# Three mantissa bits of each weight word by ScalarE into a PSUM bank, and a new table of ranks

## The chip, the core and the metric

One Trainium2 chip, one core. The metric is the device time of one execution in microseconds (us). On the core TensorE (PE) multiplies into PSUM, VectorE (DVE), ScalarE (ACT) and GpSimd (POOL) do the elementwise work, and SyncE (SP) issues nearly all the transfers. PSUM has eight banks of 512 fp32 numbers for each of 128 partitions.

## The reference, cut to what matters

```python
# attention over 32 memory rows per head: q, k, v, phi are (4, 8, 576, 64 or 32)
a = softmax(phi, axis=2)
k_m = einsum('bhsm,bhsd->bhmd', a, k);  v_m = einsum('bhsm,bhsd->bhmd', a, v)
attn = softmax(q @ k_m.T / sqrt(64));   x = (attn @ v_m) as (2304, 512)
# a gated layer, d_ff 1536; its three weights arrive as 64-bit floats
g = x @ moe_w_gate
x = (g * sigmoid(g) * (x @ moe_w_val)) @ moe_w_out
# eight experts, each token goes to the one with the highest logit
e = argmax(x @ moe2_w_gate);  out[i] = gate_w[i] * (relu(x[i] @ w1[e]) @ w2[e])
```

The first weights, `moe_w_gate`, `moe_w_val` and `moe_w_out`, are drawn as doubles. The kernel gets each as two 32-bit words and has to make an fp32 number of them. The change is in that step.

## The kernel before, in words

Every product runs in three passes: an operand is cut into a rounded high part and a rest (`cut`, line 424: the high part by ACT, line 427, the rest by DVE or POOL, line 429), and high times high, high times rest and rest times high are added in PSUM.

The program has three parts. First, for batches 0 to 3, memory rows from `phi` (tile `ph`), `k` and `v` (tile `kvraw`), then scores against `q` (tile `qt`): PE makes `kvp` (line 535), `pt` (574) and `psc` (622); DVE turns, reduces and normalises the scores (lines 643 to 672) in a tile `sA` and leaves `af`, which `cut` turns into `at`. Second, the gated layer, in 12 column groups `ft` of 128 columns in both weights: PE multiplies the weight tile `wgv` with the memory rows `tv` into `pm` (818); `cut` makes `mh` of it; PE multiplies `mh` with `at` into `pg` and `pv` (920), a pair for each half batch; DVE and ACT make the gated `sg` and `gh`; PE multiplies `gh` with the output weight `wo` into `py` (964). Third, experts in units of 288 tokens, `p` (1480 and 1520), to the end. Batches 0 and 1 go through the gated layer first, 2 and 3 after them with weights stored and reloaded.

The weights come in 36 chunks of 512 KB (24 of `wgv`, two for each column group, 12 of `wo`). SP brings a chunk into a tile `wr` (line 723), 512 pairs of words for each partition. `words` (line 726) makes 512 fp32 numbers in the tile `mag` of it:

- line 733, ACT: reads the high word as fp32 and scales it by 2^-111, so that sign, exponent and 20 mantissa bits stand three bits too far right in `mag`;
- line 735, DVE: the sign bit of `mag`, into the high word of `wr`;
- line 737, DVE: the low word of `wr` shifted right by 29 (three mantissa bits), joined with that;
- line 739, DVE: `mag` shifted left by three, joined with it, into `mag`;
- then `cut`: ACT makes the high part of the weight tile, POOL the rest.

There are four `wr` tiles and two `mag` tiles, and `wr` is free after line 739.

The order of the work on each engine is not written out. A planner (`Loom`) runs the program as threads on a model of the engines when the kernel is built, and issues an instruction when its thread is chosen; among threads that are ready on an engine the lower rank goes first. The table `RANK` holds these ranks, for loads, conversions, scores, products and so on. The planner's costs of an instruction are `on_v`, `on_v2`, `on_a`, `on_g`, `on_pe` and `on_dma`; `on_v2` marks a DVE instruction with two operands in SBUF, for which the model lets POOL and DVE slow each other. `banks` are the eight PSUM banks, and a thread that wants one waits in the plan until one is free.

Of the kernel before, what the change touches and what calls it, by code (L numbers as in the profile page):

```python
# [9 lines left out]
F32R = mybir.dt.float32r  # L10
BF16 = mybir.dt.bfloat16
I32 = mybir.dt.int32
AF = mybir.ActivationFunctionType
ALU = mybir.AluOpType
AX = mybir.AxisListType
# [3 lines left out]


RANK = {
    "gate": -427.7, "mh": -121.7, "mem": -6.5, "mem0": -3.9, "py": 225.9, "out": 216.2, "tables": 206.8, "warm": -9,
# [5 lines left out]
    "mh1": -125.4, "py1": 5.2, "turn": -32.0, "route": -35.0, "zeros": -96.4, "lists": -142.7, "marks": -35.9, "pick": 100.3,  # L28
# [3 lines left out]
}  # L32


class Event:
    def __init__(self):
        self.time, self.waiting = None, []
# [12 lines left out]
class Loom:  # L50
# [5 lines left out]
    def __init__(self, slack=0.0, look=100.0):  # L56
        self.slack, self.look, self.table, self.shared = slack, look, AF.Exp, 0.0
        self.busy = dict.fromkeys(("PE", "V", "A", "G", "SP", "DMA"), 0.0)
# [101 lines left out]
def on_v(n, half=False):  # L160
    return "V", 0.06 + n * (0.00053 if half else 0.00105)


def on_v2(n, half=False):
    return *on_v(n, half), True


def on_a(n, table=None):
    cost = 0.11 + n * 0.00104
    return ("A", cost, table) if table else ("A", cost)  # L170


def on_g(n):
    return "G", 0.3 + n * 0.0021
# [6 lines left out]
def on_dma(kb):  # L181
    return "SP", kb / 340
# [14 lines left out]
def attention_moe_moe_kernel(  # L197
# [14 lines left out]
    nc = tc.nc  # L212
# [30 lines left out]
    def bank(name):  # L243
        return ps.tile([128, 512], F32, tag="bank", name=name, bufs=8)
# [7 lines left out]
    def wraw(shape, name, dt=F32):  # L252
        return sb.tile(shape, dt, tag="wr", name=name, bufs=4)
# [4 lines left out]
    def t2k(shape, name, dt=F32):  # L258
        return sb.tile(shape, dt, tag="t2k", name=name, bufs=2)
# [69 lines left out]
    def tables():  # L329

        cap_i = sb.tile([128, 1], I32, name="cap_i")
        rg32 = sb.tile([128, NDT, E], F32, name="rg32")
        yield atts[0].phq[0]
        yield on_dma(20)
        nc.sync.dma_start(cap_i, capacity.bitcast(I32)[0:1].partition_broadcast(128))
        yield on_dma(60)
# [4 lines left out]
        yield t2k_s  # L341
        ints = t2k([128, 512], "ints", I32)
        parts, at = [], 0
# [73 lines left out]
    loom = Loom(RANK["slack"], RANK["look"])  # L417
    banks = Slots(8)
# [6 lines left out]
    def cut(src, hi, lo, n, pool=False):  # L425
        yield on_a(n)
        nc.scalar.activation(hi, src, AF.Copy)  # L427
        yield on_g(n) if pool else on_v(n)
        (nc.gpsimd if pool else nc.vector).tensor_sub(lo, src, hi.bitcast(F32))  # L429

    class Attention:
# [67 lines left out]
        def powers(self, Q):  # L499
# [4 lines left out]
            nc.vector.tensor_reduce(sums[:, 0:1], ph[:, Q], AX.X, ALU.max, negate=True)  # L504
            yield "A", 0.95, AF.Exp
            nc.scalar.activation(ph[:, Q], ph[:, Q], AF.Exp, bias=sums[:, 0:1], accum_out=sums[:, 1:2])
            yield self.ex_ready
# [92 lines left out]
        def scores(self, n):  # L600
# [48 lines left out]
            nc.vector.tensor_sub(s2, s1, m1.unsqueeze(2).to_broadcast([128, 2 * NK, MM]))  # L649
            yield on_a(2 * NB, AF.Exp)  # L650
            nc.scalar.activation(s1, s2, AF.Exp, scale=float(D) ** -0.5)
            m2 = sb.tile([128, 2 * NK], F32, tag="m1", name="m2", bufs=4)
# [65 lines left out]
    def convert(raw_ap, dst, key, chunk, kb, rank):  # L718

        yield wr_s  # L720
        raw = wraw([128, raw_ap[1], 2], "wr", I32)
        yield on_dma(kb)
        nc.sync.dma_start(raw.rearrange("p f w -> p (f w)"), raw_ap[0])
        loom.spawn(words(raw, dst, key, chunk), rank, loom.landed)

    def words(raw, dst, key, chunk):
        low, high = raw[:, :, 0], raw[:, :, 1]
        n = raw.shape[1]
        yield mag_s
        mag = sb.tile([128, n], F32, tag="mag", name="mag", bufs=2)  # L730
        val = mag.bitcast(I32)
        yield on_a(n)
        nc.scalar.activation(mag, high.bitcast(F32), AF.Copy, scale=2.0**-111)
        yield on_v2(n, True)
        nc.vector.tensor_scalar(high, val, -(1 << 31), None, ALU.bitwise_and)
        yield on_v2(n)
        nc.vector.scalar_tensor_tensor(high, low, 29, high, ALU.logical_shift_right, ALU.bitwise_or)
        yield on_v2(n)
        nc.vector.scalar_tensor_tensor(val, val, 3, high, ALU.logical_shift_left, ALU.bitwise_or)
        loom.put(wr_s)  # L740
        hi, lo = dst
        src = mag.rearrange("p (a b) -> p a b", b=hi.shape[-1]) if len(hi.shape) == 3 else mag
        yield from cut(src, hi, lo, n, pool=True)
        loom.put(mag_s)
        loom.set(wparts[key][chunk])
# [3 lines left out]
    def weights(key, rank):  # L749

        yield w8_s
        if isinstance(key, int):
            w = wtiles[0, key] = w8([128, 2, NDT, 2, 128], "wgv")
            for i in range(2):
                src = w_gv[key, i].bitcast(I32)
                yield from convert((src, NDT * 128), (w[:, 0, :, i], w[:, 1, :, i]), key, i, 524, rank)
# [951 lines left out]
    tv_ready, turn, pair = Event(), Slots(1), Slots(1)  # L1708
# [113 lines left out]
```

## Time and profile before

| | us |
|---|---|
| median of 3 runs | 704.24 |
| lowest and highest | 702.95, 707.14 |
| the profiled execution | 702.52 |
| its span, first to last instruction | 700.7 |
| PE busy in the span | 653.9 |
| DVE, ACT, POOL busy | 455.6, 366.2, 237.0 |

The profiled execution took 1.8 us more than its span. PE is busy for 93% of the span; what it is not busy with adds up to 46.8 us. [...] In a row of the order in time, brackets at the end give how long the engine stood idle before the piece and what released it.

### The profile page before, as it was taken

What the parts mean: (1) busy time and instruction counts of PE and PEld (TensorE: products, weight loads), DVE (VectorE), ACT (ScalarE), POOL (GpSimd) and SP (SyncE); (2) the same over time, 40 slices, a digit from 0 to 9 for tenths busy, and PEclk for the clock granted to TensorE, in tenths of its full rate; (3) what the DMA queues carried; (4) which work ended last, traced back from release to release, by engine and by line L of the source; (5) the groups of instructions that cost most, each with busy time, mean ns of one, the idle gap of its engine ahead of it and who ended that gap; (6) DMA issues with size and microseconds to landing.
All of it is one profiled execution on the core that took longest, in us unless ns stands there. A gap on an engine that the chain in (4) does not pass through costs nothing. (4 is left out here: it accounts for less than half of the span.)

```text
span 700.7 us, 12589 instructions
## 1 busy us (share of the span) xinstructions
PE 653.9 (93%) x4681; PEld 600.6 (86%) x4681; DVE 455.6 (65%) x948; ACT 366.2 (52%) x695; POOL 237.0 (34%) x217
## 2 busy tenths in 40 slices
PE   5399899999999899999999999999999999999993
PEld 4198698898898789889988988889899999999982
DVE  4998987499988767813624656873663854854633
ACT  4556767777477556634613743433454543743531
POOL 3444674265536222301711320004641632421302
PEclk9689899999999999999999999999999999999998
DMA  9975667677574416245933533434955856655341
GB/s 355 384 305 214 196 240 256 226 249 235 200 308 166 185 61 211 63 179 150 308 122 124 195 102 106 121 92 101 288 147 185 249 133 218 190 158 201 109 167 38
DMA packets 48737, 132.04 MB, mean 188 GB/s; under 512 B 7648, under 2 KB 16864, under 8 KB 44064
## 3 DMA queue, kind: packets, MB, share of 16 engines
q1 hardware_dynamic: 45440, 121.44, 51.1%
q0 software_dynamic: 3232, 9.74, 4.5%
q8 instruction: 39, 0.64, 0.4%
q14 instruction: 26, 0.21, 0.1%
HBM read 98.10 MB, written 33.33 MB: 188 GB/s over the span
## 5 line engine op out<-in xcount | busy, mean ns | idle before, releaser
L964 PE MATMUL py<-wo,gh 128*128 128x512 f32 x648 | 157.0, 396 | 2.4 <-POOL wo L429 2.4
L964 PEld LDWEIGHTS py<-wo,gh 128*128 128x128 f32 x648 | 120.4, 190 | 27.0 <-POOL wo L429 3.2
L429 POOL TENSOR_TENSOR gh<-sg,gh 128x288 fp32r<-128x288 f32 x96 | 84.3, 885 | 170.7 <-ACT gh L427 165.7
L1520 PE MATMUL p<-hh,w2h 128*128 128x288 f32 x768 | 113.3, 299 | 0.2 <-issue 0.2
L1480 PE MATMUL p<-xt,w1h 128*128 128x288 f32 x768 | 110.6, 297 | 0.6 <-DVE xt L429 0.6
L1520 PEld LDWEIGHTS p<-hh,w2h 128*128 128x128 f32 x768 | 104.3, 189 | 0.5 <-ACT xt L427 0.3
L1480 PEld LDWEIGHTS p<-xt,w1h 128*128 128x128 f32 x768 | 104.0, 189 | 0.9 <-DVE xt L429 0.8
L287 POOL DMA_INDIRECT out_dram<-ot,idx x24 | 54.4, 2265 | 131.0 <-DVE ot L1559 127.9
L920 PE MATMUL pg<-at,mh 128*128 128x288 f32 x576 | 95.7, 301 | 2.0 <-POOL at L429 0.7
L920 PE MATMUL pv<-at,mh 128*128 128x288 f32 x576 | 92.9, 298 | 0.0
L920 PEld LDWEIGHTS pg<-at,mh 128*128 128x128 f32 x576 | 82.3, 190 | 6.9 <-DVE mh L429 2.0
L920 PEld LDWEIGHTS pv<-at,mh 128*128 128x128 f32 x576 | 82.2, 190 | 0.8 <-issue 0.4
L429 DVE TENSOR_TENSOR mh<-pm,mh 64x512 fp32r<-64x512 f32 (+1 forms) x88 | 60.3, 685 | 24.7 <-ACT mh L427 22.8
L833 DVE SCALAR_TENSOR_TENSOR sg<-sg,pv 128x288 f32<-128x288 f32 x96 | 42.5, 449 | 40.0 <-ACT sg L830 19.9
L427 ACT ACTIVATE mh<-pm 64x512 fp32r<-64x512 f32 (+1 forms) x88 | 51.9, 590 | 24.1 <-PE pm L818 18.9
L1496 DVE SCALAR_TENSOR_TENSOR hh<-p,hh 128x288 fp32r<-128x288 f32 x64 | 28.7, 449 | 53.6 <-ACT hh L1494 52.7
L1494 ACT ACTIVATE hh<-p 128x288 fp32r<-128x288 f32 x64 | 26.2, 409 | 68.8 <-PE p L1480 62.6
L427 ACT ACTIVATE gh<-sg 128x288 fp32r<-128x288 f32 x96 | 41.7, 442 | 34.4 <-DVE sg L833 33.2
L818 PE MATMUL pm<-wgv,tv 128*128 128x256 f32 x336 | 49.2, 292 | 10.1 <-ACT wgv L427 9.0
L429 DVE TENSOR_TENSOR w2h<-w2r,w2h 128x1024 fp32r<-128x1024 f32 x36 | 43.6, 1216 | 21.7 <-ACT w2h L427 21.7
L818 PEld LDWEIGHTS pm<-wgv,tv 128*128 128x128 f32 x336 | 44.4, 195 | 14.5 <-ACT wgv L427 9.9
L1432 POOL DMA_INDIRECT xr<-x,idg x24 | 27.0, 1123 | 73.1 <-DVE idx L1343 64.0
(205 smaller groups left out, 863.8 us busy)
## 6 DMA issues: line engine op xcount, KB each, us to landing
w1r<-in_moe_w_dram SPq DMA_DIRECT2D x36, 512.0 KB
w2r<-in_moe_w_dram SPq DMA_DIRECT2D x36, 512.0 KB
wr<-in_moe_w_gv_dram SPq DMA_DIRECT2D x24, 512.0 KB
wsc<-wgv SPq DMA_DIRECT2D x12, 1024.0 KB
wgv<-wsc SPq DMA_DIRECT2D x12, 1024.0 KB
kvraw<-in_kv_dram SPq DMA_DIRECT2D x16, 640.0 KB
wr<-in_moe_w_out_dram SPq DMA_DIRECT2D x12, 512.0 KB
osc<-wo SPq DMA_DIRECT2D x6, 1024.0 KB
```

The lines of the kernel that those rows point to most:

```text
L287: ins = nc.gpsimd.indirect_dma_start(*args, **kwargs)
L427: nc.scalar.activation(hi, src, AF.Copy)
L429: (nc.gpsimd if pool else nc.vector).tensor_sub(lo, src, hi.bitcast(F32))
L818: nc.tensor.matmul(pm[:, Q * 256 : (Q + 1) * 256], tv[:, 2 * Q + hp, a, :], w[:, c, 2 * Q + hp], start=(k == 0 and n3 == 0), stop=(k == le ...
L833: nc.vector.scalar_tensor_tensor(sg, sg, 2.0**-16, pv[:, :NB], ALU.mult, ALU.mult)
L920: nc.tensor.matmul(pg[:, :NB], mh[:, a, Q, gv * 128 : gv * 128 + 128], at[:, Q, c, ns], start=(Q == 0 and n3 == 0), stop=(Q == 1 and n3 == 2),
L964: nc.tensor.matmul(py, gh[:, a, k * TC : (k + 1) * TC], wtiles[P, ws[j // 2]][:, j % 2, c, :], start=(j == 0 and n3 == 0), stop=(j == FG - ...
L1432: nc.gpsimd.indirect_dma_start(self.xr[:, c], None, x2[: NT // 2] if self.early else x2, bass.IndirectOffsetOnAxis(idg[:, c : c + 1], 0))
L1480: nc.tensor.matmul(p1[:, :NB], self.w1[d][:, a, f * 128 : f * 128 + 128], self.xt[d][:, c], start=(d == 0 and n3 == 0), stop=(d == NDT - 1 ...
L1494: nc.scalar.activation(dst[:, 0], p1[:, :NB], AF.Relu)
L1496: nc.vector.scalar_tensor_tensor(dst[:, 1], p1[:, :NB], 0.0, dst[:, 0].bitcast(F32), ALU.max, ALU.subtract)
L1520: nc.tensor.matmul(p2[:, :NB], self.w2[f // 2][:, f % 2, a, d * 128 : d * 128 + 128], self.hh[f][:, c], start=(f == 0 and n3 == 0), stop=( ...
```

## The change

In `words` three DVE instructions become two and ACT gets a second one. ACT reads the upper 16 bits of the low word as an unsigned integer (`top`, one element of 2 bytes out of each 8), scales it by 2^-13 with a bias that makes the rounding a rounding down, and writes the three bits as integers into a PSUM bank, `rest`. DVE joins the sign bit of `mag` to `rest` in PSUM, then `mag` shifted left by three with `rest` into `mag`. The `wr` tile is free when ACT has read it; the conversion holds one of the eight banks from the ACT instruction to the second DVE instruction. In the planner both DVE instructions are `on_v`. The `RANK` table is replaced as a whole, so that the order of all engines is another. The rows of the table say nothing to a reader; two stand for them.

```diff
-        low, high = raw[:, :, 0], raw[:, :, 1]
+        high = raw[:, :, 1]
...
-        yield on_v2(n, True)
-        nc.vector.tensor_scalar(high, val, -(1 << 31), None, ALU.bitwise_and)
-        yield on_v2(n)
-        nc.vector.scalar_tensor_tensor(high, low, 29, high, ALU.logical_shift_right, ALU.bitwise_or)
-        yield on_v2(n)
-        nc.vector.scalar_tensor_tensor(val, val, 3, high, ALU.logical_shift_left, ALU.bitwise_or)
+        yield banks
+        rest = bank("rest")[:, :n].bitcast(I32)
+        top = raw.rearrange("p f w -> p (f w)").bitcast(U16).rearrange("p (f w) -> p f w", w=4)[:, :, 1]
+        yield on_a(n)
+        nc.scalar.activation(rest, top, AF.Copy, bias=2.0**-14 - 0.5, scale=2.0**-13)
         loom.put(wr_s)
+        yield on_v(n)
+        nc.vector.scalar_tensor_tensor(rest, val, -(1 << 31), rest, ALU.bitwise_and, ALU.bitwise_or)
+        yield on_v(n)
+        nc.vector.scalar_tensor_tensor(val, val, 3, rest, ALU.logical_shift_left, ALU.bitwise_or)
+        loom.put(banks)
...
 RANK = {
-    "0ph": -128.5, "0kv0": -121.3, "0kv1": -56.1, "0q0": 48.4, "0q1": -118.9, "0m0": 109.9, "0m1": -64.4, "0s0": -159.6,
...
+    "0ph": -162.0, "0kv0": -136.0, "0kv1": -377.0, "0q0": 181.1, "0q1": -139.4, "0m0": 136.5, "0m1": -351.5, "0s0": -381.1,
...
```

Three places of the new order. The first is SP at the very start: `ph_105` is `phi` of batch 0, `ph_115` of batch 1, `kvraw` are the four parts of `k` and `v` of batch 0. Before:

```order
L723 DMA wr_112<-in_moe_w_gv_dram 128x1024
L723 DMA wr_121<-in_moe_w_gv_dram 128x1024
L453 DMA ph_105<-in_phi_dram 128x576 x2
L473 DMA kvraw_106<-in_kv_dram 128x1280
L473 DMA kvraw_131<-in_kv_dram 128x1280
L496 DMA qt_108<-in_q_dram 128x1152
L453 DMA ph_115<-in_phi_dram 128x576 x2
```

And now:

```order
L724 DMA wr_112<-in_moe_w_gv_dram 128x1024
L724 DMA wr_121<-in_moe_w_gv_dram 128x1024
L474 DMA kvraw_107<-in_kv_dram 128x1280
L474 DMA kvraw_125<-in_kv_dram 128x1280
L454 DMA ph_105<-in_phi_dram 128x576 x2
L497 DMA qt_108<-in_q_dram 128x1152
L474 DMA kvraw_106<-in_kv_dram 128x1280
```

Two transfers of 640 KB now stand ahead of the first `ph`.

The second is PE at the scores of batch 1 (`psc`); `pm` of the column groups 0, 1, 2 and 3 read `wgv_109`, `wgv_111`, `wgv_113` and, for group 3, `wgv_255` before and `wgv_214` now; `tv_100` is batch 0, `tv_102` batch 1. Before:

```order
L574 MATMUL pt_690<-ident_63,kvs_688 128x128 x2
L622 MATMUL psc_700<-qt_116,tk_605 64x288 x2
L622 MATMUL psc_706<-qt_116,tk_694 64x288 x2
L818 MATMUL pm_714<-wgv_109,tv_102 128x256 x12
L622 MATMUL psc_699<-qt_116,tk_605 64x288 x2
L818 MATMUL pm_733<-wgv_111,tv_102 128x256 x12
L622 MATMUL psc_747<-qt_116,tk_694 64x288 x2
L818 MATMUL pm_770<-wgv_113,tv_102 128x256 x12
L920 MATMUL pg_777<-at_387,mh_598 128x288 x6
```

And now:

```order
L575 MATMUL pt_679<-ident_63,kvs_677 128x128 x2
L623 MATMUL psc_688<-qt_116,tk_552 64x288 x2
L623 MATMUL psc_694<-qt_116,tk_683 64x288 x2
L623 MATMUL psc_687<-qt_116,tk_552 64x288 x2
L623 MATMUL psc_708<-qt_116,tk_683 64x288 x2
L823 MATMUL pm_723<-wgv_214,tv_100 128x256 x12
L823 MATMUL pm_741<-wgv_109,tv_102 128x256 x12
L925 MATMUL pg_774<-at_396,mh_740 128x288 x6
```

The last `pg` reads group 3 of batch 0: `mh_598` was made of `pm_541`, 18 rows earlier on PE, and `mh_740` is made of `pm_723`, two rows earlier.

The third is DVE at the same place; `sums` are row maxima of `ph` of batch 2, which is being loaded. Before:

```order
L643 STREAM_TRANSPOSE sA_698<-psc_700 128x288
L643 STREAM_TRANSPOSE sA_698<-psc_706 128x288
L647 TENSOR_REDUCE m1_739<-sA_698 128x18
L403 TENSOR_TENSOR rg_92<-rg32_118,rg_92 128x4x8
L649 TENSOR_TENSOR sA_698<-sA_698,m1_739 128x576
L429 TENSOR_TENSOR mh_730<-pm_714,mh_730 128x512
L504 TENSOR_REDUCE sums_717<-ph_713 128x1
L504 TENSOR_REDUCE sums_736<-ph_713 128x1
```

And now:

```order
L648 TENSOR_REDUCE m1_717<-sA_686 128x18
L644 STREAM_TRANSPOSE sA_686<-psc_687 128x288
L650 TENSOR_TENSOR sA_686<-sA_686,m1_717 128x576
L644 STREAM_TRANSPOSE sA_686<-psc_708 128x288
L505 TENSOR_REDUCE sums_712<-ph_705 128x1
L648 TENSOR_REDUCE m1_747<-sA_686 128x18
L505 TENSOR_REDUCE sums_719<-ph_705 128x1
L655 TENSOR_REDUCE m2_744<-sA_686 128x18
L430 TENSOR_TENSOR mh_740<-pm_723,mh_740 128x512
```

The `mh` that PE wants next stands behind five instructions that follow line 650, two of them on `ph` of batch 2.

## Rows read from the trace of the kernel before

**Rows 1.** The page, part 1: engine, busy us, share of the span, instructions.

```profile
PE 653.9 (93%) x4681; PEld 600.6 (86%) x4681; DVE 455.6 (65%) x948; ACT 366.2 (52%) x695; POOL 237.0 (34%) x217
```

**Rows 2.** Stretches: length, busy PE, PEld, DVE, ACT, POOL, granted clock, DMA share, GB/s.

```profile
0.00:36.00 36.00, 15.26 (x136) 11.03 (x137) 25.77 (x53) 17.50 (x36) 13.19 (x26) 0.83 0.93 371
36.00:72.00 36.00, 35.18 (x298) 31.45 (x297) 33.76 (x81) 22.30 (x45) 14.72 (x20) 0.93 0.65 243
72.00:86.00 14.00, 10.93 (x42) 8.57 (x41) 13.67 (x20) 10.99 (x19) 9.62 (x7) 0.76 0.61 198
86.00:220.00 134.00, 133.24 (x948) 119.01 (x947) 110.63 (x191) 91.78 (x187) 65.18 (x58) 1.00 0.67 240
220.00:690.00 470.00, 458.42 (x3263) 430.18 (x3262) 271.04 (x607) 223.62 (x412) 133.17 (x107) 1.00 0.50 159
```

**Rows 3.** The tile mag: least, median and greatest ns of a line's instructions.

```profile
L735 DVE TENSOR_SCALAR wr<-mag x36: 387/422/1654, 5.1 to 210.4; 128x512 int32<-128x512 int32 x36
L739 DVE SCALAR_TENSOR_TENSOR mag<-mag,wr x36: 648/693/1925, 6.3 to 217.6; 128x512 int32<-128x512 int32 x36
```

**Rows 4.** PE in order of time, from the first matmul to the first pm.

```profile
6.49 3.01 PE L1725 MATMUL warm<-ident,ph 128*128 128x128 f32 x13 [6.49 <-DMA ph<-in_phi_dram]
...
19.20 1.19 PE L622 MATMUL psc<-qt,tk 128*64 128x288 f32 x8
...
33.99 0.58 PE L818 MATMUL pm<-wgv,tv 128*128 128x256 f32 x1 [8.99 <-ACT wgv L427]
35.50 2.71 PE L818 MATMUL pm<-wgv,tv 128*128 128x256 f32 x11 [0.93 <-POOL wgv L429]
```

**Rows 5.** PE in order of time: the first of its waits from 72 us on.

```profile
75.69 0.96 PE L964 MATMUL py<-wo,gh 128*128 128x512 f32 x3 [1.59 <-POOL wo L429]
```

**Rows 6.** Groups of instructions on DVE: count, busy us, mean ns, idle before.

```profile
L739 DVE SCALAR_TENSOR_TENSOR mag<-mag,wr 128x512 int32<-128x512 int32 x36 | 33.4, 931 | 0.9
L737 DVE SCALAR_TENSOR_TENSOR wr<-wr 128x512 int32<-128x512 int32 x36 | 33.1, 921 | 0.4
L735 DVE TENSOR_SCALAR wr<-mag 128x512 int32<-128x512 int32 x36 | 21.3, 595 | 4.9 <-ACT mag L733 4.7
L429 DVE TENSOR_TENSOR mh<-pm,mh 64x512 fp32r<-64x512 f32 x80 | 54.8, 686 | 24.7 <-ACT mh L427 22.8 <-issue 0.4
```

**Rows 7.** DVE and POOL in order of time, one instruction each at 26 us.

```profile
26.76 1.57 DVE L739 SCALAR_TENSOR_TENSOR mag<-mag,wr 128x512 int32<-128x512 int32 x1
...
26.09 1.68 POOL L429 TENSOR_TENSOR wgv<-mag,wgv 128x512 fp32r<-128x512 f32 x1 [2.73 <-ACT wgv L427]
```

**Rows 8.** Groups of instructions on ACT, from SBUF and from PSUM.

```profile
L733 ACT ACTIVATE mag<-wr 128x512 f32<-128x512 f32 x36 | 23.9, 668 | 12.9 <-DMA wr<-in_moe_w_gv_dram 6.7 <-POOL wgv L429 5.3 <-DMA wr<-in_moe_w_out_dram 0.8
L427 ACT ACTIVATE mh<-pm 64x512 fp32r<-64x512 f32 x80 | 47.2, 589 | 20.0 <-PE pm L818 15.2 <-PE pv L920 1.9 <-DVE mh L429 1.4
```

**Rows 9.** ACT in order of time: the second and the third weight chunk landing.

```profile
5.65 0.68 ACT L733 ACTIVATE mag<-wr 128x512 f32<-128x512 f32 x1 [0.56 <-DMA wr<-in_moe_w_gv_dram]
...
17.92 0.67 ACT L733 ACTIVATE mag<-wr 128x512 f32<-128x512 f32 x1 [0.71 <-DMA wr<-in_moe_w_gv_dram]
```

**Rows 10.** PE in order of time at the scores of batch 1.

```profile
59.19 0.44 PE L574 MATMUL pt<-ident,kvs 128*128 128x128 f32 x2 [0.82 <-DVE kvs L557]
59.56 1.19 PE L622 MATMUL psc<-qt,tk 128*64 128x288 f32 x8
60.68 1.69 PE L818 MATMUL pm<-wgv,tv 128*128 128x256 f32 x12
```

**Rows 11.** DVE in order of time at the same place.

```profile
62.34 0.76 DVE L649 TENSOR_TENSOR sA<-sA,m 128x576 f32<-128x576 f32 x1
63.04 0.69 DVE L429 TENSOR_TENSOR mh<-pm,mh 128x512 fp32r<-128x512 f32 x1
...
65.34 0.75 DVE L504 TENSOR_REDUCE sums<-ph 128x1 f32<-128x576 f32 x1 [0.95 <-DMA ph<-in_phi_dram]
```

**Rows 12.** Line 735 alone in two stretches: length, busy DVE with count, clock, DMA share, GB/s.

```profile
0.00:86.00 86.00, 8.16 (x15) 0.86 0.76 289
```

More of the change, by code (lines that the diff above doesn't have):

```diff
@@ L12 @@
 I32 = mybir.dt.int32
+U16 = mybir.dt.uint16
 AF = mybir.ActivationFunctionType
@@ L21 @@
 RANK = {
-    "gate": -427.7, "mh": -121.7, "mem": -6.5, "mem0": -3.9, "py": 225.9, "out": 216.2, "tables": 206.8, "warm": -9,
[5 rows of a table removed]
-    "mh1": -125.4, "py1": 5.2, "turn": -32.0, "route": -35.0, "zeros": -96.4, "lists": -142.7, "marks": -35.9, "pick": 100.3,
[3 rows of a table removed]
+    "gate": -386.6, "mh": -144.3, "mem": -5.8, "mem0": 13.9, "py": 352.3, "out": 15.0, "tables": 401.6, "warm": -9,
[5 rows of a table added]
+    "mh1": -393.3, "py1": 4.1, "turn": -479.2, "route": 51.5, "zeros": -397.0, "lists": -145.9, "marks": -148.5, "pick": -84.9,
[3 rows of a table added]
 }
```

14 rows, old and new, of the table RANK are left out of this document.

## The prediction

> **What bounds the kernel now.** I read the shares of the engines first, then the busy time by stretches, then the opening in order of time. TensorE is busy for 653.9 of 700.7 us [rows 1], so 46.8 us of idle time, and the time at the low clock, are all that a change off PE can win. The stretches say where it lies [rows 2]: 20.7 us before 36 us, 0.8 from 36 to 72, 3.1 from 72 to 86, 0.8 from 86 to 220, 11.6 from 220 to 690, and the tail of some 10 us behind that. The 36 conversions end before 220 us (the last line 739 starts at 217.6) [rows 3], so those 11.6 us and the tail have no conversion in them. DVE is the fullest engine where the conversions are: 33.8 of 36 us and 13.7 of 14 us in the second and third stretch, but 110.6 of 134 in the fourth, where PE hardly waits. So a DVE that is 83% full costs PE next to nothing there, and what the change can win on the path lies in the first 86 us.
>
> [...] The first `pm` waits 9.0 us for ACT and 0.9 for POOL, until 35.5 [rows 4]; both are the end of a conversion, whose middle is DVE. From 72 to 86 PE waits for POOL's cuts, of `wo` first [rows 5] and then of `at`, together 14 - 10.93 = 3.1 us. [...]
>
> **The change part by part.** *Engine time.* Removed on DVE: 21.3 + 33.1 + 33.4 = 87.8 us in 36 chunks [rows 6], 2.44 us a chunk. Added: 72 instructions of 128x512 with one operand in PSUM. The row that does nearest to this, `mh`, takes 686 ns [rows 6]; the dearest near one, line 739, 931 ns. No DVE instruction of the trace writes PSUM, so both ends stay. I take 686, since like the new ones it has one operand in SBUF only: 49.4 us, a saving of 38.4 us, 1.07 a chunk (at 931 it is 20.8 us and 0.58). The high mean of the old lines is not their own: alone line 739 takes 693 [rows 3], but beside a POOL cut it took 1.57 us, and the cut 1.68 [rows 7]. Both old joins read SBUF twice; the new ones don't, so POOL's cuts should come down too. Added on ACT: 36 instructions of 589 (from PSUM) to 668 ns (strided, from SBUF) [rows 8]; I take 668: 24 us, on an engine that is 52% busy. A conversion alone is no shorter: 0.67 + 0.42 + 2 x 0.69 before (the medians) [rows 3, 8], 2 x 0.67 + 2 x 0.69 now, 0.25 more; the gain is only DVE's room for others.
>
> The row for a PSUM operand (686) and the row without one (693) do not differ [rows 3, 6]. [...]
>
> *The opening.* The new table puts two `kvraw` transfers, 1.31 MB, ahead of the first `ph`. From the second to the third landed chunk, 5.65 to 17.92 us [rows 9], the queue brought 4.91 MB, 0.40 MB a us, so `ph` lands 3.3 us later. PE's start waits for just that transfer (6.49 us) [rows 4], and `warm`, exp, memory rows and scores of batch 0 follow it: the first `psc` moves from 19.2 to 22.5. Behind it DVE has the scores and, as before, the conversions up to the sixth chunk, which the first `pm` needs in both orders. One more of them now falls behind the first scores, so four conversions of 1.38 stand in place of three of 2.44: 5.5 against 7.3 us. By itself that would bring the sixth chunk 1.8 us earlier; ACT's second instruction and the waits for one of the two `mag` tiles take some of it, so I count 0.9. The first `pm` is 3.3 - 0.9 = 2.4 us **later**, at 37.9 (between 1.0 and 3.3).
>
> *To the scores of batch 1.* From there PE has the same work in both orders, without a wait that DVE sets except the 0.8 us for `kvs` [rows 10], which a freer DVE may spare or not: 0 to -0.8, I take -0.4. One `pm` group (1.7 us) [rows 10] now comes behind the scores and not ahead of them, so `psc` starts at 59.6 + 2.4 - 0.4 - 1.7 = 59.9, about where it was.
>
> *A new wait.* Behind the scores PE has twice the former `psc` (2.4 us) and two `pm` (3.3), and is through at 65.6. It then wants `mh_740`, of the first of these `pm`. In the new order its cut stands behind the exp of the scores on ACT, and on DVE behind line 650 and five more. Line 649 ended 3.5 us after the scores began (59.6 to 63.1) [rows 10, 11], now one turning later, 63.9; then a turning and four reductions, each like the one of 0.75 or less [rows 11], 3.4 together, until 67.3 (the second of them on `ph` waited for its transfer until 65.3 before, which is covered), and 0.7 for `mh`: 68.0. PE waits 2.4 us (1.0 if the two halves overlap better, 3.5 if the tenth chunk, of `wgv_214`, is late). Queued behind it are all of `pg`, `sg` and `gh`.
>
> *What goes away.* `at` of batch 1 is now behind scores without any conversion between them, and `wo` isn't wanted before all of the first two batches' `pg` of four column groups, nine pairs of `pg` and `pv` later in the new order. So the 3.1 us of waits and the 3.2 us of low clock from 72 to 86 go: -6.3.
>
> *Behind 86 us.* PE waits 0.8 us while the other 21 conversions run: at most -0.8, I take 0. The order there is another too; 11.6 us of small waits from 220 on may shift by 2 us either way, and the last units stand in the same order as before: 0.
>
> Sum: 2.4 - 0.4 + 2.4 - 6.3 = **-1.9 us**. Against the profiled execution, 702.52, that is 700.6; that execution lies 1.7 us below the median of the runs, 704.24, which gives 702.3. I say **702**.
>
> **The rivals.** *The freed DVE carries through* (faster). The opening loses only its lower end (1.0), the new wait is 1.0, `kvs` doesn't wait, and the small waits give 1.4: 1.0 + 1.0 - 0.8 - 1.4 - 6.3 = -6.5, 697.7. For it: DVE is full up to 86 us and loses 15 x 1.07 = 16 us there (15 of the 36 conversions start line 735 before 86) [rows 12]. Against it: the chain through `ph` has no DVE in it.
>
> [...]
>
> *The eighth bank* (slower). Each conversion holds a bank for 0.67 + 2 x 0.69 us at least, and longer where DVE has other work between. PE takes a new bank for each group of six matmuls, every 0.84 us (133.24 / 948 for one [rows 2]). If half of the 21 chunks behind 86 us hold PE up by one DVE instruction (0.69), that is +7.2 on my 702.3: 709.5. It decides where DVE is behind, and DVE's load there falls from 110.6 to 88 of 134 us, which speaks against it. [...]
>
> *The joins are dearer* (the change doesn't do what it says): 931 ns or more where DVE writes PSUM. Six conversions of the opening then cost 12 x 0.25 = 3 us more, and the first `pm` comes later by that: 702.3 + 3 = 705.3.
>
> **How the numbers follow.** My forecast 0.34 (its own range 700 to 704.5), carried through 0.32, clock 0.16, bank 0.10, dearer joins 0.08. A measurement here tells about 0.5%, 3.5 us, from no change: faster is below 700.7, slower above 707.8. Faster: 0.32 and 0.05 of my own case, 0.37. Slower: the bank and a third of the clock's case, 0.16. Same: 0.47. The range takes the carried-through case and the clock's upper end: 697 to 708.
>
> **What would show it.** Lines 742 and 744 near 0.69 us with hardly any above 0.8, line 739 of after (on ACT) at 0.6 to 0.67; `warm` at 9.8 us and the first full `pm` near 38; a wait of `pg` for `mh` at 65 to 69 us; no wait for `wo`, and a granted clock of 1 from 72 to 86. It is wrong if the first `pm` comes before 35.5, if the clock falls again near 70, or if PE waits between 86 and 220 us for banks (a release by line 744).

## The result, and the profile after

| | before | changed |
|---|---|---|
| median of 4 runs | 705.69 | 696.67 |
| lowest and highest | 702.95, 707.16 | 695.82, 699.12 |
| the profiled execution, and its span | 702.52, 700.7 | 696.09, 694.3 |

The ratio is **0.9882 (95% interval 0.9838 to 0.9927)**: about 1.2% faster. In later runs (e11) beside the kernel before it was 0.9859 (0.9827 to 0.9891). The forecast was 702, no change, with a range of 697 to 708; the time lies 0.3 below its lower end, and the case that came true is the first rival, "the freed DVE carries through" (697.7).

The page of the changed kernel, part 1, answers to [rows 1]:

```profile
PE 649.9 (94%) x4681; PEld 599.9 (86%) x4681; DVE 420.0 (60%) x912; ACT 381.7 (55%) x729; POOL 229.1 (33%) x217
```

DVE has 35.6 us less, POOL 7.9 less, ACT 15.5 more. The stretches, with the columns of [rows 2]:

```profile
0.00:36.00 36.00, 14.69 (x133) 10.82 (x133) 19.35 (x42) 18.84 (x39) 9.63 (x17) 0.90 0.97 382
36.00:72.00 36.00, 30.45 (x255) 27.39 (x256) 28.29 (x77) 23.28 (x47) 17.10 (x29) 0.87 0.56 204
72.00:86.00 14.00, 14.00 (x112) 14.00 (x111) 9.68 (x20) 13.30 (x30) 9.06 (x9) 1.00 0.52 172
86.00:220.00 134.00, 134.00 (x943) 119.32 (x942) 94.70 (x171) 105.44 (x209) 61.18 (x61) 1.00 0.70 258
```

PE is worse off up to 72 us (30.45 busy in the second stretch against 35.18). From 72 us on it doesn't wait at all, at full clock, where before it waited 3.1 us, had a clock of 0.76 to 86 us, and waited 0.8 more to 220. The new lines, and POOL's cut, in the view of a tile as in [rows 3]:

```profile
L739 ACT ACTIVATE rest<-wr x36: 600/627/657, 5.1 to 208.0; 128x512 int32<-128x512 uint16 x36
L742 DVE SCALAR_TENSOR_TENSOR rest<-mag,rest x36: 661/693/697, 5.7 to 209.3; 128x512 int32<-128x512 int32 x36
L744 DVE SCALAR_TENSOR_TENSOR mag<-mag,rest x36: 643/684/689, 6.4 to 212.3; 128x512 int32<-128x512 int32 x36
L430 POOL TENSOR_TENSOR wgv<-mag,wgv x24: 1261/1290/1307, 7.9 to 200.5; 128x512 fp32r<-128x512 f32 x24
```

None of the 72 joins took over 0.70 us, where the old ones reached 1.9 [rows 3]. PE in order of time, the waits up to 86 us (as [rows 4, 5, 10]):

```profile
9.99 3.01 PE L1730 MATMUL warm<-ident,ph 128*128 128x128 f32 x13 [9.99 <-DMA ph<-in_phi_dram]
...
23.63 1.19 PE L623 MATMUL psc<-qt,tk 128*64 128x288 f32 x8
...
38.30 0.58 PE L823 MATMUL pm<-wgv,tv 128*128 128x256 f32 x1 [11.75 <-ACT wgv L428]
39.65 5.28 PE L823 MATMUL pm<-wgv,tv 128*128 128x256 f32 x23 [0.77 <-POOL wgv L430]
...
64.86 3.02 PE L823 MATMUL pm<-wgv,tv 128*128 128x256 f32 x23 [1.08 <-POOL wgv L430]
...
69.32 0.80 PE L925 MATMUL pg<-at,mh 128*128 128x288 f32 x4 [1.17 <-DVE mh L430]
```

The opening is 4.1 us later than before (39.65 against 35.50), the foreseen new wait is there in two pieces (1.08 and 1.17), and `wo` is waited for nowhere.

**A mark of equal work.** The order differs, so equal times are not equal progress. But ahead of the first `pw` (the first turning of finished `rows` of the gated layer) PE has the same 1465 matmuls in every kernel here, a filler not counted. That `pw` starts at 230.3 us before and at 225.7 after:

```profile
L1013 PE MATMUL pw<-ident,rows x72: 271/273/332, 230.3 to 443.5; 128*128 128x128 f32 x72
```

```profile
L1018 PE MATMUL pw<-ident,rows x72: 270/272/329, 225.7 to 437.6; 128*128 128x128 f32 x72
```

So of the 6.4 us between the two first spans 4.6 lie ahead of the first `pw`, where all conversions are, and 1.8 behind it. For each run I give PE's idle time up to the first `pw`, and what PE gave away there at the low clock: its busy time in each stretch of 1 us times (1 - granted clock), summed. The granted clock is a share of full speed; in stretches of 1 us up to 188 us it is 1.00 or 0.50 in every trace here, but for those at the ends of a low stretch. The first full `pm` is the first group of `pm` that starts when POOL's rest of the weights is there.

| run | ratio, 95% interval | span | first full `pm` | PE idle | given away by clock | first `pw` | behind it |
|---|---|---|---|---|---|---|---|
| before | 1 | 700.7 | 35.50 | 26.9 | 6.7 | 230.3 | 470.4 |
| before again (e12) | 1.0012 (0.9979 to 1.0045) | 703.5 | 35.56 | 27.0 | 4.8 | 228.7 | 474.8 |
| changed | 0.9882 (0.9838 to 0.9927) | 694.3 | 39.65 | 26.9 | 3.2 | 225.7 | 468.6 |
| changed again (e11) | 0.9859 (0.9827 to 0.9891) | 691.9 | 38.43 | 27.3 | 3.2 | 224.5 | 467.4 |
| e1 new order, old words | 0.9988 (0.9963 to 1.0013) | 699.8 | 40.61 | 33.0 | 2.5 | 232.9 | 466.9 |
| e2 old order, new words | 0.9889 (0.9865 to 0.9914) | 693.5 | 34.65 | 23.3 | 2.0 | 221.7 | 471.8 |
| e3 rest in SBUF | 0.9927 (0.9908 to 0.9946) | 698.5 | 40.71 | 31.0 | 3.4 | 231.0 | 467.5 |
| e4 first join twice | 0.9999 (0.9978 to 1.0020) | 701.8 | 42.13 | 34.3 | 2.4 | 235.0 | 466.8 |
| e8 ACT twice | 0.9956 (0.9937 to 0.9975) | 700.2 | 40.66 | 30.2 | 3.1 | 230.3 | 469.9 |
| e5 ph first | 0.9856 (0.9827 to 0.9885) | 691.6 | 37.49 | 23.8 | 3.5 | 223.5 | 468.1 |
| e6 filled | 0.9866 (0.9839 to 0.9892) | 694.9 | 40.08 | 20.2 + 7.2 | 3.8 | 225.2 | 469.7 |
| e7 ph first, filled | 0.9809 (0.9781 to 0.9838) | 690.3 | 37.19 | 15.7 + 7.9 | 1.6 | 220.7 | 469.6 |
| e9 before, filled | 0.9974 (0.9950 to 0.9998) | 701.0 | 36.97 | 19.7 + 8.1 | 3.2 | 230.1 | 470.9 |
| e10 e2, filled | 0.9861 (0.9828 to 0.9893) | 688.8 | 34.74 | 15.4 + 8.1 | 0.0 | 220.5 | 468.3 |

(In the filled runs, those with matmuls that nobody reads in a wait of PE, the second number is the filler's.) Idle time, filler and what the clock took, subtracted from the first `pw`, leave 194 to 199 us in all of them; the spread is that of rows whose ends are modelled. The two traces of before differ by 4.4 us behind the first `pw`, so single spans tell no more than that, and small differences are read from the ratios.

### The profile page after: what moved, and what is told of

The parts are those of the page before. It is cut to its first block, busy times and chain, and to the rows that moved or that the text cites. A ratio compares the mean times of both kernels' runs of the same rounds, so it can differ in the third digit from the quotient of the medians.

```text
span 694.3 us, 12547 instructions
## 1 busy us (share of the span) xinstructions
PE 649.9 (94%) x4681; PEld 599.9 (86%) x4681; DVE 420.0 (60%) x912; ACT 381.7 (55%) x729; POOL 229.1 (33%) x217
## 5 line engine op out<-in xcount | busy, mean ns | idle before, releaser
L969 PE MATMUL py<-wo,gh 128*128 128x512 f32 x648 | 154.6, 392 | 0.0
L430 POOL TENSOR_TENSOR gh<-sg,gh 128x288 fp32r<-128x288 f32 x96 | 79.4, 831 | 163.5 <-ACT gh L428 154.1
L1437 POOL DMA_INDIRECT xr<-x,idg x24 | 29.3, 1221 | 72.7 <-DVE idx L1348 64.8
```

What stands on the lines that cost most here:

```text
L969: nc.tensor.matmul(py, gh[:, a, k * TC : (k + 1) * TC], wtiles[P, ws[j // 2]][:, j % 2, c, :], start=(j == 0 and n3 == 0), stop=(j == FG - ...
L1437: nc.gpsimd.indirect_dma_start(self.xr[:, c], None, x2[: NT // 2] if self.early else x2, bass.IndirectOffsetOnAxis(idg[:, c : c + 1], 0))
```

## The experiments

### Words or order: e1 and e2

Both halves of the change by themselves. In e1 the new order stays instruction for instruction, and the old three operations stand in the new places:

```diff
-        high = raw[:, :, 1]
+        low, high = raw[:, :, 0], raw[:, :, 1]
...
         yield on_a(n)
-        nc.scalar.activation(rest, top, AF.Copy, bias=2.0**-14 - 0.5, scale=2.0**-13)
         loom.put(wr_s)
         yield on_v(n)
-        nc.vector.scalar_tensor_tensor(rest, val, -(1 << 31), rest, ALU.bitwise_and, ALU.bitwise_or)
+        nc.vector.tensor_scalar(high, val, -(1 << 31), None, ALU.bitwise_and)
+        nc.vector.scalar_tensor_tensor(high, low, 29, high, ALU.logical_shift_right, ALU.bitwise_or)
         yield on_v(n)
-        nc.vector.scalar_tensor_tensor(val, val, 3, rest, ALU.logical_shift_left, ALU.bitwise_or)
+        nc.vector.scalar_tensor_tensor(val, val, 3, high, ALU.logical_shift_left, ALU.bitwise_or)
```

> The new table's order of all engines is kept instruction for instruction; only the arithmetic of a conversion is the old one (three operations on DVE, none of them with an operand in PSUM, nothing extra on ACT). Theory W (the words pay: DVE's room): what was won goes again. Each conversion has 2.4 us on DVE and not 1.4, so the first full pm comes 2 us or more behind the 39.65 us of the changed kernel, PE's wait for mh near 69 us grows from 1.2 to 3 us or more, and DVE is late again behind 86 us: 703 to 708 us, a ratio of 0.997 to 1.004 to the kernel before. Theory O (the order pays: nine pairs of pg and pv ahead of the first py): no wait for wo and no low clock from 72 to 86 us whatever the words cost, and the time stays within 1.5 us of the changed kernel: 695 to 698, a ratio of 0.985 to 0.990.

Measured: 702.56, a ratio of 0.9988 (0.9963 to 1.0013). The stretches of e1:

```profile
36.00:72.00 36.00, 28.44 (x243) 25.40 (x244) 31.17 (x79) 20.19 (x41) 18.25 (x29) 0.87 0.60 215
72.00:86.00 14.00, 14.00 (x113) 14.00 (x113) 11.40 (x24) 11.90 (x26) 7.66 (x7) 1.00 0.44 159
86.00:220.00 134.00, 130.51 (x906) 114.44 (x905) 114.45 (x190) 87.94 (x177) 60.74 (x57) 1.00 0.71 256
```

The order alone does take the waits and the low clock out of 72 to 86 us, just as theory O says, and yet wins nothing: PE waits 3.5 us between 86 and 220 us instead, and the opening is 5 us late. Theory W holds in the time, not in all its marks: the first full `pm` came 1.0 us later than in the changed kernel and not 2 or more, and the wait for `mh` stayed at 1.17 us.

In e2 the old order stays, with the new words in it:

```diff
-        low, high = raw[:, :, 0], raw[:, :, 1]
+        high = raw[:, :, 1]
...
         nc.scalar.activation(mag, high.bitcast(F32), AF.Copy, scale=2.0**-111)
+        rest = bank("rest")[:, :n].bitcast(I32)
+        top = raw.rearrange("p f w -> p (f w)").bitcast(U16).rearrange("p (f w) -> p f w", w=4)[:, :, 1]
+        nc.scalar.activation(rest, top, AF.Copy, bias=2.0**-14 - 0.5, scale=2.0**-13)
         yield on_v2(n, True)
-        nc.vector.tensor_scalar(high, val, -(1 << 31), None, ALU.bitwise_and)
         yield on_v2(n)
-        nc.vector.scalar_tensor_tensor(high, low, 29, high, ALU.logical_shift_right, ALU.bitwise_or)
+        nc.vector.scalar_tensor_tensor(rest, val, -(1 << 31), rest, ALU.bitwise_and, ALU.bitwise_or)
         yield on_v2(n)
-        nc.vector.scalar_tensor_tensor(val, val, 3, high, ALU.logical_shift_left, ALU.bitwise_or)
+        nc.vector.scalar_tensor_tensor(val, val, 3, rest, ALU.logical_shift_left, ALU.bitwise_or)
```

> The old table's order is kept on every engine; only the arithmetic of a conversion is the new one (ScalarE's second operation stands right behind its first, the two joins stand where the two old joins stood, the place of the sign is empty, and the bank is taken without a place in the plan). Theory W: the saving shows without the new order. The first full pm comes 1.8 us ahead of the 35.50 of before, the wait for wo at 74 to 77 us (2.4) falls below 0.8 since each conversion is 1 us shorter on DVE, and rows no longer come 1.6 us late at 230 us: 697 to 700 us, a ratio of 0.988 to 0.993. Theory O: the waits for wo and at from 72 to 86 us stay, since POOL's cuts end them, the clock falls there again, and the time stays at 703 to 706, a ratio of 0.996 to 1.001. A third way, the bank rival: PE waits for a bank where a rest holds it, over 707.

Measured: 695.61, a ratio of 0.9889 (0.9865 to 0.9914), the whole gain without the new order. The first full `pm` is 0.85 us ahead of before, not the 1.8 that theory W gave it. PE of e2 at the first `py`, in order of time, and its stretch:

```profile
70.04 2.68 PE L967 MATMUL py<-wo,gh 128*128 128x512 f32 x10 [0.43 <-DVE mag L742]
73.51 0.73 PE L967 MATMUL py<-wo,gh 128*128 128x512 f32 x2 [0.79 <-POOL wo L430]
74.88 0.93 PE L923 MATMUL pg<-at,mh 128*128 128x288 f32 x5 [0.51 <-POOL at L430]
```

```profile
72.00:86.00 14.00, 12.39 (x58) 9.67 (x58) 9.20 (x16) 13.01 (x24) 8.91 (x7) 1.00 0.71 242
```

Three waits again, 1.7 us where before had 3.1 (1.59, 0.79 and 0.70), and the clock stays at full speed. POOL still ends the second and the third. The first of before, 1.59 for a cut of `wo`, is gone. POOL at this place, before and then in e2:

```profile
71.92 2.03 POOL L429 TENSOR_TENSOR gh<-sg,gh 128x288 fp32r<-128x288 f32 x2 [10.14 <-ACT gh L427]
73.91 3.47 POOL L429 TENSOR_TENSOR wo<-mag,wo 128x512 fp32r<-128x512 f32 x2
```

```profile
68.89 1.56 POOL L430 TENSOR_TENSOR gh<-sg,gh 128x288 fp32r<-128x288 f32 x2 [9.82 <-ACT gh L428]
70.41 3.05 POOL L430 TENSOR_TENSOR wo<-mag,wo 128x512 fp32r<-128x512 f32 x2
```

In both POOL cuts here without a break, so its cut of `wo` was not waiting for a join; the four cuts took 5.5 us before and 4.6 in e2, longer beside the old joins as in [rows 7]. Up to the first `pw` e2 wins 8.6 us on the first trace of before, 7.0 on the second: 3.6 or 3.7 of idle time (1.5 of it the wait for `rows` at 230 us, which is gone), 4.7 or 2.8 of clock. The 0.43 us is ended by the last join, whose result that `py` does not read. I take it for a wait for the bank that a `rest` held, of which this plan knows nothing; it is the only wait in this trace that a line of the joins ends.

The two tables meet with the same words at 0.9889 against 0.9882 and 0.9859, with the old words at 1 against 0.9988: **the new order is worth nothing that these runs can tell; the words are worth it all**. In these traces the order costs 2.6 to 4.2 us ahead of the first `pw` (its opening) and has some 3 less behind it (466.9 to 468.6 against 470.4 to 474.8); over all traces of the table the two ranges behind `pw` overlap (466.8 to 469.9 with the new order, 468.3 to 474.8 with the old).

### What the words' gain is made of: e3, e4 and e8

e3 keeps the instructions and the order, and puts the three bits over the high words in SBUF, the memory in which the other tiles of a conversion lie:

```diff
-        rest = bank("rest")[:, :n].bitcast(I32)
+        rest = high
```

> The changed kernel with its order kept; ScalarE writes the three bits over the high words in SBUF, not into a bank of PSUM, so both joins have two operands in SBUF as the old ones had, and the raw tile is freed behind the last join. The count of instructions is the changed kernel's. Theory P (one operand in PSUM spares the join): lines 742 and 744 go from a mean of 0.69 us back to 0.8 to 0.95, some above 1.5 beside a POOL cut, and POOL's wgv cuts go from 1.29 to 1.35 and more; DVE's busy time rises from 420 by 8 to 17 us, and the time by 1 to 4: 698 to 701, a ratio of 0.989 to 0.994. Rival (there is one instruction less, and where its operands lie is all the same): means of 0.69, and the time within 1 us of the changed kernel, a ratio of 0.986 to 0.990. [...]

Measured: 698.58, 0.9927 (0.9908 to 0.9946). Groups of e3 on DVE and POOL: count, busy us, mean ns, idle before:

```profile
L744 DVE SCALAR_TENSOR_TENSOR mag<-mag,wr 128x512 int32<-128x512 int32 x36 | 29.5, 821 | 1.3
L742 DVE SCALAR_TENSOR_TENSOR wr<-mag,wr 128x512 int32<-128x512 int32 x36 | 27.9, 781 | 24.2 <-ACT wr L739 23.9
```

```profile
L430 POOL TENSOR_TENSOR wgv<-mag,wgv 128x512 fp32r<-128x512 f32 x24 | 33.6, 1402 | 42.9 <-ACT wgv L428 42.6
```

Means of 0.82 and 0.78 (0.68 and 0.69 with the bank), single ones of 1.65, and POOL's cut back at its 1.40 of before: theory P. It costs 0.0045 to 0.0068 against the changed kernel, 3 to 5 us. One thing goes with it: `wr` is free only behind the last join, one `kvp` waits 1.4 us for its transfer, and ACT is busy for 168.1 us up to the first `pw` and not 166.3, with 332 instructions in both; so the 3 to 5 are an upper bound for the operand alone. DVE's busy time rose by 7.3 us, a little less than the 8 to 17 expected.

e4 puts DVE time back, in the conversions themselves:

```diff
         nc.vector.scalar_tensor_tensor(rest, val, -(1 << 31), rest, ALU.bitwise_and, ALU.bitwise_or)
+        nc.vector.scalar_tensor_tensor(rest, val, -(1 << 31), rest, ALU.bitwise_and, ALU.bitwise_or)
```

> The changed kernel with its order kept, but line 742 is issued twice in each conversion (the second gives the same bits again). That puts 36 x 0.69 = 25 us back on DVE, two thirds of the 38 that the change takes off it, and nothing else. Theory W: DVE's room is what pays, so some two thirds of the 9 us come back: 700 to 704 us, a ratio of 0.993 to 0.998. Theory O: the order carries it; the opening's first pm comes 0.7 to 2 us later and the rest is hidden: 697 to 699, a ratio of 0.988 to 0.991.

Measured: 703.39, 0.9999 (0.9978 to 1.0020). The 25 us take back all of the gain, more than either theory had; the idle time ahead of the first `pw` goes from 26.9 to 34.3. That is 8 to 10 us of time for 25 of DVE.

e8 does the same on ACT:

```diff
         nc.scalar.activation(rest, top, AF.Copy, bias=2.0**-14 - 0.5, scale=2.0**-13)
+        nc.scalar.activation(rest, top, AF.Copy, bias=2.0**-14 - 0.5, scale=2.0**-13)
```

> The changed kernel with its order kept, but ScalarE's second operation (line 739) issued twice in each conversion, with the same result: 36 x 0.63 = 23 us more on ACT, which is at 381.7 of 694 us, and the bank is held that much longer. The prediction counted the first 24 us on ACT as free behind the opening. Theory A (ACT has the room): the first pm comes 0.6 to 1.5 us later, nothing else: 697 to 699, a ratio of 0.988 to 0.991. Theory B (an operation in front of a chain that ends on POOL costs the same whichever engine has it): it costs what the same length did on DVE, where 25 us gave 6.7: 701 to 704, a ratio of 0.994 to 0.998.

Measured: 701.97, 0.9956 (0.9937 to 0.9975): 23 us on an engine that is 55% busy cost 5 to 7 us, theory B in its numbers; a microsecond costs some 0.7 of what it cost on DVE. The first full `pm` is 1 us later than in the first trace of the changed kernel and the first `pw` 4.6. Both e4 and e8 also make each conversion longer by the instruction that they add, so they price time inside a conversion; they don't tell an engine's room from the conversion's length.

### The opening and its clock: e5, e6, e7, e9, e10

e5 puts `ph` back ahead of the two `kvraw`, e6 fills PE's wait ahead of the first `pm`, e7 does both:

```diff
-    "0ph": -162.0, "0kv0": -136.0, "0kv1": -377.0, "0q0": 181.1, ...
+    "0ph": -162.0, "0kv0": -136.0, "0kv1": -161.0, "0q0": 181.1, ...
```

```diff
                 yield on_pe(6 * len(hps), 256)
+                if bs == (0,) and ft == 0:
+                    fill = bank("fill")
+                    for _ in range(64):
+                        nc.tensor.transpose(fill[:, :128], ident, ident)
                 project(...)
```

> The changed kernel with one number of its table changed (0kv1 from -377 to -161), so that the two transfers of phi stand ahead of the two kvraw of the second half, as in the kernel before; else four rows of PE's order move, all ahead of the scores of batch 0. Theory A (the transfers' order sets the opening, as the prediction had it: 3.3 us on ph, carried on to the first pm): warm starts at 6.5 to 6.9 us and not at 9.99, the first full pm at 36 to 37.5 and not at 39.65, and 2 to 3 us of the total go: 693.5 to 695, a ratio of 0.983 to 0.986. Theory B (the first pm is set by the weight chunks' landing and by DVE behind the scores, whatever ph does): warm comes early, the first full pm stays at 39 or later, and the time is the changed kernel's within 1 us: a ratio of 0.986 to 0.990.

Measured: 693.38, 0.9856 (0.9827 to 0.9885). `warm` starts at 6.45, and of the 3.5 us that this is earlier, 0.9 to 2.2 reach the first full `pm` (37.49 against 38.43 and 39.65) and 1.0 to 2.2 the first `pw`. The mark is at the edge of theory A; in the ratio it can't be told from the changed kernel.

> The changed kernel with its order kept, and 64 transposes of the unit matrix on TensorE, read by nobody, ahead of the first pm, where TensorE otherwise waits 11.75 us. They take some 10 us of that wait if each takes what a px takes in the trace (0.16). Theory A (the low clock behind the wait is on the path): the granted clock stays at 1.0 through the first pm, the 23 pm behind the first take 3.1 us and not 5.28, the 3.2 us that PE loses by the low clock up to 46 us go, and 1.5 to 3 us of the total: 694 to 695.5, a ratio of 0.984 to 0.987. Theory B (mh, on ACT and DVE behind the scores, ends last there anyway): the clock stays up but the first pg starts at 47 us as now, and the time is within 1 us of the changed kernel: a ratio of 0.987 to 0.990. If the transposes run longer than the wait, the first pm comes later by the rest.

Measured: 695.98, 0.9866 (0.9839 to 0.9892). PE of e6 in order of time:

```profile
26.88 7.21 PE L883 MATMUL fill<-ident 128*128 128x128 f32 x64
38.73 0.58 PE L823 MATMUL pm<-wgv,tv 128*128 128x256 f32 x1 [4.64 <-ACT wgv L428]
40.08 4.59 PE L823 MATMUL pm<-wgv,tv 128*128 128x256 f32 x23 [0.76 <-POOL wgv L430]
```

The filler was too short (0.113 us each, not 0.16). PE idled 4.64 us behind it, the clock was at 0.5 again when `pm` came, and 2.1 us were given away there (3.2 without the filler); the other 1.7 of its 3.8 lie at 16 to 20 us, ahead of the filler. The theories were not told apart here; e7 does more.

> Both at once: the two transfers of phi ahead, and the 64 unread transposes ahead of the first pm. If both theories A hold, the gains add: 690.5 to 693 us, a ratio of 0.979 to 0.982 to the kernel before, which beats both kernels. If the first pm comes so early that the transposes outlast the wait, the second gain shrinks to 0 to 1 us: a ratio of 0.982 to 0.985. If theory B holds in both, 0.986 to 0.990.

Measured: 691.79, **0.9809 (0.9781 to 0.9838)**, the fastest version here: clearly ahead of the kernel before, and ahead of the changed one by 0.005 to 0.007, where the intervals just meet or overlap.

```profile
27.28 7.92 PE L883 MATMUL fill<-ident 128*128 128x128 f32 x64
35.84 0.38 PE L823 MATMUL pm<-wgv,tv 128*128 128x256 f32 x1 [0.64 <-ACT wgv L428]
37.19 3.02 PE L823 MATMUL pm<-wgv,tv 128*128 128x256 f32 x23 [0.96 <-POOL wgv L430]
```

Here the filler ends 0.64 us ahead of `pm`, the clock is full, and the 23 `pm` take 3.02 us and not 5.28. The first `pw` is 2.8 us ahead of e5's and the ratio 0.0047 below it. The intervals overlap by 0.0011, but all five times of e7 (688.92 to 692.32) lie below all five of e5 (692.86 to 696.58): the low clock of the opening was on the path. The 1.6 us that e7 still gives away lie at 25 to 29 us, ahead of the filler and in it.

The same with the old order, 72 transposes: e9 with the old words, e10 with the new.

> The kernel before, order and words, with 72 transposes of the unit matrix on TensorE, read by nobody, ahead of the first pm, in the 9.0 us that TensorE waits there; at the 0.11 us that one took in the run with 64 they last 8.1. This takes the low clock at the first pm by itself, without the words. Theory A (the 3.5 us that the kernel before loses by the low clock from 34 to 41 us are on the path, and belong to the conversions' length only through the wait): the clock is 1.0 there, and 1.5 to 3.5 us of the total go, a ratio of 0.995 to 0.998. Theory B (the conversions behind it are late anyway, with DVE 33.8 of 36 us busy): the first pm group is faster and PE waits longer behind it: a ratio of 0.998 to 1.002.

Measured: 702.13, 0.9974 (0.9950 to 0.9998). The time is as theory A has it, but not by its way. The first `pm` came at 35.46 and not 33.99, the filler ended 4.04 us ahead of it, and the opening gave away 3.2 us at the low clock, nearly its 3.5. What is missing in this trace is the low clock from 78 us on; the first wait for `wo` was 0.95 us there and not 1.59. It is not the chance of one execution: the granted clock over the whole span was 0.987 in the mean of its 12 runs, against 0.978 in the runs of before beside them (0.989 and 0.980 in the two traces). Why the filler should shorten that wait stays open.

> The old table's order with the new words, and 72 unread transposes ahead of the first pm. Theory A: with the new words DVE is no longer in the way, so the 2.0 us of PE time lost at the low clock from 33 to 38 us go: 1 to 2 us below the run without them, a ratio of 0.986 to 0.9875. Theory B: no change against that run, 0.988 to 0.991. If the new table is worth nothing beside the new words once the transfers of phi stand first, this comes out at the 0.981 of the new order with phi first and filled; if the new order is worth its 2 to 4 us behind the first pw, that one stays ahead by 0.003 to 0.006.

Measured: 693.57, 0.9861 (0.9828 to 0.9893). Nothing is given away by the clock any more, and the first `pw` is 1.2 us ahead of e2's; the step in the ratio (0.0028) is no larger than the intervals. Against e7 (0.9809) the ratio would make the new order worth some 0.005 once its opening is mended, but the intervals overlap and the two traces show no such gap (first `pw` at 220.5 and 220.7, spans 688.8 and 690.3), so that is not shown.

### The scale: e11 and e12

> The changed kernel as it is, again, on the chip and beside the runs of before that the last experiments use, as the scale of the smaller differences: a ratio of 0.985 to 0.991, and a trace in which the first full pm starts within 0.7 us of 39.65, the first pw within 1.5 us of 225.7. If these marks move by more, differences of 2 us between single traces mean nothing.

Measured: 693.86, 0.9859. The first `pw` is 1.2 us earlier and the first full `pm` 1.2, more than the 0.7 I allowed. So a difference of 1 or 2 us at one mark between two single traces, as in e5, says little by itself.

> The kernel before as it is, for a second trace: a ratio of 0.998 to 1.002, the two waits for wo from 74 to 78 us and the low clock behind them again, the first full pm within 0.7 us of 35.5 and the first pw within 1.5 us of 230.3. If the low clock from 78 to 85 us is missing, it is chance and can't be counted in what the words win.

Measured: 706.16, 1.0012 (0.9979 to 1.0045). The first full `pm` is where it was (35.56), the first `pw` 1.6 us earlier, a little more than I allowed. The stretch of e12:

```profile
72.00:86.00 14.00, 10.92 (x46) 8.66 (x45) 13.63 (x20) 10.97 (x19) 9.36 (x7) 0.88 0.61 203
```

Both waits for `wo` are there again, and so is the low clock, but for half as long (1.6 us given away, not 3.1). So the low clock is there in both traces of before, but its length is chance.

## Why the prediction was right or wrong

**What bounds the kernel: wrong.** "A DVE that is 83% full costs PE next to nothing there, and what the change can win on the path lies in the first 86 us" is the step that failed, and with it the 0 that I took behind 86 us. What the runs show in its place: in e1, with nearly the same DVE load (114.45 of 134 us), PE waits 3.5 us there, and in the changed kernel, with the same order (94.70), none. That it didn't show in [rows 2] because other things were late first in the old order is my reading, not shown. Beyond 220 us `rows` came 1.57 us late for the first `pw`. The last conversion had left DVE 10.8 us before `rows` began there, and yet the wait is gone where the words alone are changed (e2); I had counted it among the 11.6 us that "have no conversion in them". With the 0.5 us of waits at 162 and 169 us that is 2.1 us up to the first `pw`, and 1.8 of the 6.4 lie behind it (within what two traces of one kernel differ by).

**What goes away: the size right, the cause wrong.** From 72 to 86 us the waits (3.1) and the low clock (3.1) went, 3.1 + 3.1 = 6.2 against the 6.3 priced. No run shows the 3.2 us of low clock in that sum as such: the trace of before has a granted clock of 0.50 from 78.3 to 85.1 us and gives away the 3.1 there, the second trace (e12) 1.6. But I gave waits and clock to the order. e1 shows that the order takes them away, e2 that the words do so without it, all the clock and 1.4 us of the waits. Each half of the change was enough, so the term belongs to neither alone, and a sum over parts could not show that.

**DVE's time: right.** 0.69 and 0.68 us a join, 35.6 us saved against 38.4 worked out. That the joins last longer, up to 1.65 us, when both operands lie in SBUF, and POOL's cuts of `wgv` with them (1.40 us in the mean against 1.29), is shown by e3. "The joins are dearer" is out.

**ACT's time: the size right, its cost wrong.** 0.63 us an instruction as predicted (0.60 to 0.67). I let 24 us of it cost only a part of the opening's 0.9; e8 puts 5 to 7 us on as much again. Since the DVE time that goes is worth 8 to 10 us for each 25 (e4), the net is an estimate of 36 x 0.36 - 22 x 0.26 = 7 us, near the measured 8 to 10.

**The opening: right in place, under-sized in the first trace.** `warm` at 9.99 (9.8 predicted), the first `psc` at 23.63 (22.5), the first full `pm` at 39.65 and 38.43 (37.9): 4.1 and 2.9 us later than in the two traces of before, where I had 2.4 and at most 3.3. The saving by the words there is 0.85 in e2, as I took (0.9); the 3.3 us on `ph` became 4.4 at `psc`. e5 says that only 0.9 to 2.2 us of the delay of the first full `pm` are due to the transfers' order.

**The new wait: right.** 1.08 + 1.17 = 2.25 us at 64 to 69 us (2.4 predicted), partly for `wgv` and not for `mh` alone. `kvs` isn't waited for (-0.8; -0.4 predicted).

**The rivals.** The clock (0.16: that the new wait would bring it down, the upper end of the range) didn't fall: it was 1.00 from 46 us on, through the waits of 1.08 and 1.17 us. No bank was waited for: no wait of PE ended with line 744, and PE is busy for 134.00 of the 134 us from 86 to 220. The freed DVE carried through, though not by the sum that I gave it (opening +1.0, small waits -1.4): the opening lost 3 to 4, and more came back behind 86 us. My argument against it, "the chain through `ph` has no DVE in it", looked at the one place where the change loses.

**The sum on the first two traces:** opening +4.1, `kvs` -0.8, new wait +2.3, 72 to 86 us -6.2, from 86 us to the first `pw` -2.1, behind it -1.8: -4.5 of the 6.4. The other 1.9 lie in gaps too small for the list of waits and in modelled ends, and stay open. The table says it more simply for this pair: ahead of the first `pw` PE idles 26.9 us in both kernels, what the new order loses in the opening and the new wait being what is won behind them, and 3.5 of the 4.6 us are those no longer given away at the low clock. The medians differ by 9.0 us, more than one pair of traces shows.

## What to carry to other kernels

Where a change has two halves, such as new instructions and a new order, run each alone on the other's ground; here the part that a reading of waits credited with the gain was worth nothing by itself. Time on an engine that is not the fullest is not free if the work lies in a chain (here 25 us on DVE, 60% busy, cost 8 to 10, and 23 us on ACT, 55% busy, 5 to 7): price a microsecond there by issuing an instruction twice that gives the same result. And where DVE and POOL work side by side, look for two-operand DVE instructions with both operands in SBUF, and put one of them into PSUM if a bank can be had: here the joins' means were 0.69 and 0.68 us with a bank and 0.78 and 0.82 without (e3).

## What the runs showed of the hardware

**DVE beside POOL.** In the changed kernel a join with one operand in PSUM lay beside a POOL cut, but for its last 0.06 us, and took its usual time; DVE first, then POOL, in order of time:

```profile
56.74 0.70 DVE L742 SCALAR_TENSOR_TENSOR rest<-mag,rest 128x512 int32<-128x512 int32 x1
```

```profile
56.08 1.30 POOL L430 TENSOR_TENSOR wgv<-mag,wgv 128x512 fp32r<-128x512 f32 x1
```

A tiny DVE instruction, SBUF to SBUF, beside another such cut did not:

```profile
38.52 1.10 DVE L657 TENSOR_SCALAR m<-m 128x18 f32<-128x18 f32 x1
```

```profile
38.33 1.27 POOL L430 TENSOR_TENSOR wgv<-mag,wgv 128x512 fp32r<-128x512 f32 x1 [1.17 <-ACT wgv L428]
```

Six of the eight in this trace take 0.13 to 0.18 us; this one ended with the cut, at 39.6, and the eighth, 1.22 us long at 161 us, with another. Where both operands of the joins lie in SBUF (e3), single joins took up to 1.65 us and POOL's cuts of `wgv` up to 1.81, where with a bank none took over 0.70 and 1.31. What held up the two tiny instructions is not shown by a run.

**A PSUM operand costs DVE nothing here.** The joins took 690 and 680 ns on average with one, and in the median 693 and 684; without one the medians were 692 and 693 (e3). ACT writes the three bits to PSUM in 0.625 us, 36 times; with its output in SBUF (e3) ACT was busy for 1.8 us more up to the first `pw` (168.05 against 166.28), with 332 instructions in both, an estimate of 0.05 us more for each.

**The clock.** Where PE idled 4.6 or 4.0 us behind a filler (e6, e9) the granted clock was 0.5 at the next full `pm`; where it idled 0.64 or 1.26 (e7, e10) it was 1. The waits of 0.43, 0.79 and 0.51 us at 70 to 75 us left it at 1 (e2), and so did those of 0.95, 0.77 and 0.69 at 76 to 80 us in e9; with those of 1.6, 0.8 and 0.7 it was 0.5 in both traces of before, from 78.3 to 85.1 us in the first and from 78.6 to 82.0 in the second.
